# Row sums in three pieces and a routing spread over VectorE's gaps, in an RWKV attention and mixture-of-experts kernel

## The chip, the cores and the metric

The kernel runs on one core of a Trainium2 chip. The metric is the device time of one execution in microseconds (us); lower is better.

## The reference

An RWKV attention of 4 batches, 8 heads, 768 steps and head dimension 48 feeds a mixture of 8 experts, of which each row takes one.

```python
for t in range(S):                      # B, H, S, D = 4, 8, 768, 48
    cur = einsum('bhd,bhe->bhde', u[None] * k[t], v[t])
    y[t] = einsum('bhd,bhde->bhe', r[t], state + cur)
    state = w[t][..., None] * state + einsum('bhd,bhe->bhde', k[t], v[t])
x = y as (3072, 384) rows
logits = x @ w_gate + modality_bias[modality_id]
e_idx = argmax(logits); gate = softmax(logits)[e_idx]
out[row] = gate[row] * (relu(x[row] @ w1[e_idx]) @ w2[e_idx])     # 384 -> 1024 -> 384
```

## The kernel before

The attention works in 24 units of 128 steps, six for each batch. `att_iter(i)` writes one software-pipelined iteration: VectorE prepares keys and rows of unit a = i+2, TensorE makes scores and state of unit m = i+1 and outputs of unit z = i, and the finished rows of unit z-1 are added up and carried on. The tile framework schedules by hand here (`manual_schedule`): the order in which the program issues instructions is the order of each engine's queue, and the framework adds the semaphores.

In one iteration VectorE runs, in this order: a scan over the decays backwards (`scan(pp, -1)`, L356), the row sum (`x_rows`, `x_add`, L525: output pY of unit z-1 plus the diagonal term dV, 128x384, into `xp`), K of unit a (`spread`, L330), a reciprocal and a copy of four columns (L405, L406), the scan forwards, R of unit a (L330, both in `rows_op`), and the mask of the scores (L449, pS into A).

TensorE runs: transposes of K (`k_turn`, L420) unless unit m is the last of its batch; transposes of the rows of unit z-2 (`x_halves`, L550); the scores pS (L447); `delta(m)` (L342, the diagonal term, which ends with ScalarE's copy dT, L344); the state pU (L470) unless m is the last of its batch; `logits(z-2)` (L555); the state's part of the output pY (L490) unless z is the first of its batch; the unit's own part (L501). Where m is the last of its batch, the logits stand behind L490.

ScalarE copies the transposed keys (KT, L423) and rows (xT, L435), copies dT, makes half of dV (L377), scales the state (L473) and copies it to SPb (L476). GpSimd makes products of the inputs (L293, L298, L310) and the other half of dV (L370).

There is one buffer each for pS, pY and pK. The bank `T["R"]` (pR in the page) is shared: its first 192 columns hold the logits of all units, behind them stand the routing's columns, and from column 504 on the output of delta.

The routing goes in two parts, of 10 and 14 units (`PART`). The first runs inside the attention: `route_a(0)` is a generator of six VectorE operations on logits (L596 to L606), `route_x` ScalarE's exponential, `route_b` the matmuls that count rows, then `place` (positions of six units, L642), the sum of the exponentials (L637) and its reciprocal (L638), and `table(0)`. They are started from a list `hooks`, one entry an iteration, in iterations 11 to 14; a hook's VectorE operations come behind the iteration's mask. For units n with `far(n)`, which are 10 to 13 (`PART[0] <= n <= SCATTER`), the row sum is done in another way: ScalarE copies pY to `xp` (L536) and GpSimd adds dV in place (L525); that falls in iterations 11 to 14.

From iteration 15 on GpSimd scatters the routed rows (L759), in iteration 20 SP loads the first block of rows, and behind the attention the expert blocks follow.

Of the kernel before, what the change touches and what calls it, by code (L numbers as in the profile page):

```python
# [18 lines left out]
P = 128  # L19
# [50 lines left out]
NPW = 3  # L70
LOAD = SCATTER + 1 + NEAR
# [3 lines left out]
def kernel(ctx: ExitStack, tc: tile.TileContext, rkw, vt, wf, cst, mid, wg, bias, w1, w2, out):  # L75
# [270 lines left out]
    hooks = []  # L346
# [11 lines left out]
    def rows_op(a):  # L358
        step["second", a - 2] = scan(pw[a % NPW], 1)
        spread(a, "R", ins[a % NIN][:, 0:512], 1, 3)  # L360
# [11 lines left out]
    def att_iter(i):  # L372
# [28 lines left out]
        if ok(z - 1) and not far(z - 1):  # L401
            x_rows(z - 1)
        if ok(a):
            spread(a, "K", t[:, 512:1024], 3)
            nc.vector.reciprocal(out=pp[:, 1:n:SEG], in_=BE[:, 2:n:SEG])  # L405
            nc.vector.tensor_copy(out=W, in_=BE[:, 2:n:SEG])  # L406
        if i == NU - 1:
            blk_turn(0, (2,))
# [32 lines left out]
        if ok(m):  # L441
            A = wt(m, "A", [P, 2, 4, P])
            pS = pq.tile([P, 2, 4, P], F32, tag="pS", name=f"pS_{m}")
            for p in range(4):
                for hh in range(2):
                    q = slice(64 * hh, 64 * hh + 64)
                    nc.tensor.matmul(out=pS[:, hh, p], lhsT=K[q, p], rhs=R[q, p], start=True, stop=True)  # L447
            a2 = lambda v: v.rearrange("p a b c -> p (a b) c")
            step["mask", i] = nc.vector.tensor_tensor(out=a2(A), in0=a2(pS), in1=mask[:, None, :].to_broadcast([P, H, P]), op=ALU.mult)  # L449
            if i == -1:  # L450
                rows_op(a)
            if m == 0:
                k_turn()
                k_copy()
            delta(m)
            if m == 0:
                warm(NWARM[2])
# [20 lines left out]
        if ok(z - 2) and not late:  # L478
            logits(z - 2)
# [17 lines left out]
        if ok(z):  # L497
            for h in range(H):
                p, hh = divmod(h, 2)
                for q in (0, 64):  # L500
                    nc.tensor.matmul(out=pY[q:q + 64, h * D:(h + 1) * D], lhsT=A[:, hh, p, q:q + 64], rhs=v[:, h * D:(h + 1) * D],  # L501
                                     start=(first(z) and h == 0), stop=True, skip_group_check=True)
        if i == NU - 2:
# [17 lines left out]
    def far(n):  # L521
        return PART[0] <= n <= SCATTER

    def x_add(n, eng, y):
        eng.tensor_tensor(out=T["xb", n][:, 0:DM], in0=y, in1=T["dV", n].rearrange("p a b -> p (a b)"), op=ALU.add)  # L525

    def x_rows(n, eng=None):
# [5 lines left out]
        if eng is None:  # L533
            x_add(n, nc.vector, y)
# [54 lines left out]
    def route_a(c):  # L589
# [6 lines left out]
        nc.vector.scalar_tensor_tensor(out=lg, in0=lg, scalar=-1.0, in1=biasT[:, units(c)], op0=ALU.mult, op1=ALU.subtract)  # L596
        mx = wt(c, "mx", [P, NMOST], 1)[:, 0:n]
        nc.vector.tensor_reduce(out=mx, in_=lg, axis=AX.X, op=ALU.min)
        nc.vector.tensor_tensor(out=rcol(C_RK, n, E + 1)[:, :, 1:E + 1], in0=lg, in1=mx[:, :, None].to_broadcast(sh), op=ALU.is_equal)
        yield  # L600
        eq, flat = rcol(C_RK, n, E + 1), lambda t: t[:, 0:n].rearrange("p a b -> p (a b)")
        nc.vector.tensor_tensor_scan(out=flat(seen), data0=flat(same), data1=rcol(C_RK, n * (E + 1)), initial=0.0, op0=ALU.mult, op1=ALU.max)
        oh = T["oh", c] = wt(c, "oh", [P, NMOST, E], 2, BF16)[:, 0:n]
# [13 lines left out]
    def route_b(c):  # L617
# [16 lines left out]
        if c == 0:  # L634
            place(0, NEAR)
        sm = wt(c, "sm", [P, NMOST, 1], 1)[:, 0:n]
        nc.vector.tensor_reduce(out=sm, in_=ex[:, 0:n], axis=AX.X, op=ALU.add)  # L637
        nc.vector.reciprocal(out=T["xp", c][:, :, DM:DM + 1], in_=sm)  # L638
# [303 lines left out]
    for i in range(-2, NU):  # L942
# [5 lines left out]
        if i == PART[0] + 1:  # L948
            ra, tb = route_a(0), table(0)
            hooks.extend([lambda: next(ra), lambda: [*ra], lambda: hook_b(0), lambda: [*tb]])  # L950
# [55 lines left out]
    x_rows(NU - 1)  # L1006
# [259 lines left out]
```

## Time and profile before

| | |
|---|---|
| median of 3 runs | 333.1 us (332.62 to 334.82) |
| profiled execution | 335.17 us, span 333.4 us |
| mean granted TensorE clock | 0.997 |
| busy share of the span: PE, PEld, DVE, ACT, POOL | 96%, 89%, 71%, 62%, 48% |
| DVE row sums in `x_add` | 20, each 128x384 |
| attention, until the first expert matmul | 0 to 118.72 us of the span |

PE is TensorE's matmuls, PEld its weight loads, DVE is VectorE, ACT ScalarE, POOL GpSimd and SP the engine that issues loads. Times in rows are microseconds from the span's start. A row of a timeline has the start, the duration, the engine, the line and operation, output <- inputs, and the count of merged instructions; in brackets is idle time ahead of it and what ended it. The pitch of two rows is the difference of their starts. Ends of matmuls are modelled.

### The profile page before, as it was taken

Reading aid. Unit: us, or ns where it says so; the run is one execution under the profiler, and the core shown is the slowest. Engines: PE = TensorE matmul, PEld = TensorE weight load, DVE = VectorE, ACT = ScalarE, POOL = GpSimd, SP = SyncE. Lnnn points to the kernel's source line nnn. Section 1 sums busy time; section 2 is a strip of 40 time slices with the busy share of each in tenths; the row PEclk is TensorE's granted clock in tenths of the full one; section 3 lists DMA queues with packets and bytes.
Section 4 is the critical chain, followed back from the end, with each engine's and each line's share of the span. In section 5 each row is a group of like instructions: output and inputs, shape, how many; then the busy total and the mean of one; then the engine's idle time right before and its main releaser. Section 6 shows DMA issues by size and latency. Waiting matters only on the chain.

```text
span 333.4 us, 10270 instructions
## 1 busy us (share of the span) xinstructions
PE 321.6 (96%) x3917; PEld 297.6 (89%) x3917; DVE 236.2 (71%) x508; ACT 206.3 (62%) x516; POOL 159.6 (48%) x196
## 2 busy tenths in 40 slices
PE   7999999999999999999799999999999999999993
PEld 3689999889999987899589999999999988999982
DVE  7999999999999684794459758858258445815510
ACT  1687688687799893552359456956956944614420
POOL 7899999999998177065561200210210220121031
PEclk9999999999999999999999999999999999999998
DMA  7998988888984702426844800540650653210011
GB/s 237 397 297 273 272 271 280 267 256 253 283 255 133 154 3 95 97 95 237 247 158 122 261 24 2 121 162 2 128 182 3 209 129 96 94 73 21 0 32 55
DMA packets 38735, 52.31 MB, mean 157 GB/s; under 512 B 19189, under 2 KB 26133, under 8 KB 38676
## 3 DMA queue, kind: packets, MB, share of 16 engines
q1 hardware_dynamic: 35572, 42.09, 42.7%
q0 software_dynamic: 3104, 9.47, 7.6%
q8 instruction: 33, 0.54, 0.7%
q14 instruction: 26, 0.21, 0.3%
HBM read 55.43 MB, written 11.88 MB: 202 GB/s over the span
## 4 chain that ended last, share of the span: by engine, by line
issue 42%; PE 34%; POOL 11%; DVE 5%; POOLq 2%; DMA 2%; ACT 1%; SPq 1%; DVEq 0%
POOL out L870 7%; PE pS L447 6%; PE pY L501 5%; PE pS_u L827 5%; PE pY L490 4%; PE pR_x L342 3%; POOL xs L759 3%; PE pU L470 3%; PE pR_x L555 2%; POOLq L1075 2%; DMA cs<-cst 1%; PE pY_d L848 1%; DVE wl L288 1%; PE pR_x L142 1%; SPq L120 1%
## 5 line engine op out<-in xcount | busy, mean ns | idle before, releaser
L870 POOL DMA_INDIRECT out<-ot,xg x25 | 27.3, 1091 | 132.8 <-ACT ot L869 130.7
L832 DVE SCALAR_TENSOR_TENSOR hl<-pS_u,hh 128x512 fp32r<-128x512 f32 (+2 forms) x56 | 34.6, 619 | 64.9 <-ACT hh L831 51.2
L827 PE MATMUL pS_u<-xh,wh 128*128 128x512 f32 (+2 forms) x168 | 61.8, 368 | 1.8 <-DVE hl L832 1.8
L831 ACT ACTIVATE hh<-pS_u 128x512 fp32r<-128x512 f32 (+2 forms) x56 | 30.3, 541 | 52.1 <-PE pS_u L827 49.6
L827 PE MATMUL pS_u<-xh,wl 128*128 128x512 f32 (+2 forms) x168 | 61.4, 365 | 0.0
L288 DVE TENSOR_TENSOR wl<-raw,wh 128x768 fp32r<-128x768 f32 x52 | 48.5, 957 | 2.3 <-ACT wh L287 1.6
L287 ACT CAST wh<-raw 128x768 fp32r<-128x768 f32 (+1 forms) x60 | 44.9, 785 | 0.0
L827 PE MATMUL pS_u<-xo,wh 128*128 128x512 f32 (+2 forms) x168 | 43.4, 366 | 0.0
L848 PE MATMUL pY_d<-wh,hh 128*128 128x384 f32 x112 | 37.8, 338 | 0.0
L759 POOL DMA_INDIRECT xs<-xp,posT x24 | 26.6, 1107 | 23.5 <-DVE posT L642 19.7
L848 PE MATMUL pY_d<-wh,hl 128*128 128x384 f32 x112 | 37.7, 337 | 0.0
L848 PE MATMUL pY_d<-wl,hh 128*128 128x384 f32 x112 | 37.7, 336 | 0.0
L827 PEld LDWEIGHTS pS_u<-xh,wh 128*128 128x128 f32 x168 | 31.6, 188 | 5.4 <-DVE hl L832 2.2
L356 DVE TENSOR_TENSOR_SCAN pX_s<-pw,pX_s 128x268 f32<-128x268 f32 x48 | 34.3, 715 | 1.2 <-POOL pw L293 0.3
L827 PEld LDWEIGHTS pS_u<-xo,wh 128*128 128x128 f32 x168 | 31.0, 188 | 3.7 <-DVE xo L813 0.4
L827 PEld LDWEIGHTS pS_u<-xh,wl 128*128 128x128 f32 x168 | 31.6, 188 | 3.1
L298 POOL TENSOR_TENSOR G<-in 128x512 f32<-128x512 f32 x24 | 31.1, 1296 | 0.0
L377 ACT ACTIVATE dV<-v,dT 128x48 f32<-128x48 f32 x120 | 29.7, 327 | 0.2 <-POOL dV L370 0.2
L449 DVE TENSOR_TENSOR A<-pS,cs 128x1024 f32<-128x1024 f32 x24 | 29.2, 1218 | 0.6 <-PE pS L447 0.6
L447 PE MATMUL pS<-R,K 64*128 64x128 f32 x384 | 27.2, 281 | 1.4 <-DVE R L324 1.1
L310 POOL TENSOR_TENSOR in<-in 128x512 f32<-128x512 f32 (+1 forms) x23 | 28.2, 1227 | 0.6
L848 PE MATMUL pX_d<-wh,hh 128*128 128x384 f32 x80 | 27.0, 338 | 0.0
(322 smaller groups left out, 667.4 us busy)
## 6 DMA issues: line engine op xcount, KB each, us to landing
raw<-w SPq DMA_DIRECT2D x24, 768.0 KB
in<-rkw SPq DMA_DIRECT2D x66, 256.0 KB
v<-vt SPq DMA_DIRECT2D x24, 192.0 KB
wg<-wf SPq DMA_DIRECT2D x8, 576.0 KB
raw<-w SPq DMA_DIRECT2D x16, 192.0 KB
xs<-zt SPq DMA_DIRECT2D x12, 193.0 KB
xq<-xs SPq DMA_DIRECT2D x12, 192.0 KB
xq<-xs SPq DMA_DIRECT2D x12, 144.0 KB
```

What stands on the lines that cost most here:

```text
L287: nc.scalar.copy(out=wh[k][:, sl], in_=raw[k][:, sl])
L288: (eng or (nc.vector, nc.gpsimd)[k]).tensor_tensor(out=wl[k][:, sl], in0=raw[k][:, sl], in1=wh[k][:, sl].bitcast(F32), op=ALU.subtract)
L298: nc.gpsimd.tensor_tensor(out=G, in0=t[:, 0:512], in1=t[:, 512:1024], op=ALU.mult)
L356: return nc.vector.tensor_tensor_scan(out=BE[:, ::way], data0=pp[:, ::way], data1=d1[:, ::way], initial=0.0, op0=ALU.mult, op1=ALU.max)
L377: nc.scalar.activation(out=dV[:, h], in_=v0[:, h], func=AF.Copy, scale=dT[:, h:h + 1])
L447: nc.tensor.matmul(out=pS[:, hh, p], lhsT=K[q, p], rhs=R[q, p], start=True, stop=True)
L759: rows_apart("xs", nc.gpsimd.indirect_dma_start(out=xs[:, :], out_offset=bass.IndirectOffsetOnAxis(ap=posT[:, n:n + 1], axis=0), in_=T["xb ...
L827: nc.tensor.matmul(out=pp, lhsT=wsrc[0][:, g, c * P:(c + 1) * P], rhs=xsrc[:, c, 0:w], start=(n == 0), stop=(n == 3 * KC - 1))
L831: nc.scalar.activation(out=hh, in_=pp, func=AF.Relu)
L832: nc.vector.scalar_tensor_tensor(out=hl, in0=pp, scalar=0.0, in1=hh.bitcast(F32), op0=ALU.max, op1=ALU.subtract)
L848: nc.tensor.matmul(out=X["y", q, j][0:r1 - r0], lhsT=hsrc[:, r0:r1], rhs=wsrc[1][:, f], start=(f == 0 and n == 0), stop=(f == FC - 1 and n ...
L870: ins = nc.gpsimd.indirect_dma_start(out=out[:, :], out_offset=bass.IndirectOffsetOnAxis(ap=xg[0:m, j, 1:2].bitcast(I32), axis=0), in_=ot[ ...
```

## The change

1. The row sum of 384 columns is cut in three pieces of 128 (`XCUTS`). `x_third` issues one piece at each of three places: behind the first scan, ahead of the second scan (behind the reciprocal and the copy), and behind the second scan. The last two iterations, which prepare no further unit, keep the whole sum.
2. `far` becomes `PART[0] < n <= SCATTER`: unit 10's sum goes back to VectorE, in pieces; units 11 to 13 stay with ScalarE and GpSimd.
3. In iterations 12 to 14, where VectorE has no row sum, nine operations of the first routing take the three places (`slots`): in 12 the three up to the comparison, in 13 the scan, the one-hot and the subtraction, in 14 the positions, the sum and the reciprocal. The hooks of iterations 11 and 12 become empty; `route_b` (now matmuls alone for the first part) and the table keep theirs.
4. In those iterations `delta(m)` and `logits(z - 2)` are issued at the end, behind L501.

```diff
@@
+XCUTS = tuple((c, c + P) for c in range(0, DM, P))
...
@@ def rows_op(a):
         step["second", a - 2] = scan(pw[a % NPW], 1)
+        x_third(2)
         spread(a, "R", ins[a % NIN][:, 0:512], 1, 3)
@@ def att_iter(i):
         if ok(z - 1) and not far(z - 1):
-            x_rows(z - 1)
+            thirds.extend(x_rows(z - 1, cuts=XCUTS if ok(a) else ((0, DM),)))
+        if i in slots:
+            thirds.extend(slots[i])
+        x_third(0)
         if ok(a):
             spread(a, "K", t[:, 512:1024], 3)
             nc.vector.reciprocal(out=pp[:, 1:n:SEG], in_=BE[:, 2:n:SEG])
             nc.vector.tensor_copy(out=W, in_=BE[:, 2:n:SEG])
+            x_third(1)
...
-            delta(m)
+            if i not in slots:
+                delta(m)
...
-        if ok(z - 2) and not late:
+        if ok(z - 2) and not late and i not in slots:
             logits(z - 2)
...
+        if i in slots:
+            delta(m)
+            logits(z - 2)
         if i == NU - 2:
...
     def far(n):
-        return PART[0] <= n <= SCATTER
+        return PART[0] < n <= SCATTER
...
+    thirds = []
+
+    def x_third(k):
+        if thirds:
+            thirds.pop(0)()
...
         if eng is None:
-            x_add(n, nc.vector, y)
+            return [functools.partial(x_add, n, nc.vector, y, *c) for c in cuts]
...
@@ def route_a(c):
         nc.vector.scalar_tensor_tensor(out=lg, in0=lg, scalar=-1.0, in1=biasT[:, units(c)], op0=ALU.mult, op1=ALU.subtract)
+        if c == 0:
+            yield
         mx = wt(c, "mx", [P, NMOST], 1)[:, 0:n]
         nc.vector.tensor_reduce(out=mx, in_=lg, axis=AX.X, op=ALU.min)
+        if c == 0:
+            yield
...
         nc.vector.tensor_tensor_scan(out=flat(seen), data0=flat(same), data1=rcol(C_RK, n * (E + 1)), initial=0.0, op0=ALU.mult, op1=ALU.max)
+        if c == 0:
+            yield
...
@@ def route_b(c):
-        if c == 0:
-            place(0, NEAR)
-        sm = wt(c, "sm", [P, NMOST, 1], 1)[:, 0:n]
-        nc.vector.tensor_reduce(out=sm, in_=ex[:, 0:n], axis=AX.X, op=ALU.add)
-        nc.vector.reciprocal(out=T["xp", c][:, :, DM:DM + 1], in_=sm)
+        if c:
+            gates_sum(c)
+            gates_put(c)
...
@@
             ra, tb = route_a(0), table(0)
-            hooks.extend([lambda: next(ra), lambda: [*ra], lambda: hook_b(0), lambda: [*tb]])
+            hooks.extend([lambda: None] * 2 + [lambda: hook_b(0), lambda: [*tb]])
+            for k in range(2):
+                slots[i + 1 + k] = [functools.partial(next, ra)] * 3
+            slots[SCATTER + 1] = [functools.partial(place, 0, NEAR), functools.partial(gates_sum, 0), functools.partial(gates_put, 0)]
```

`gates_sum` and `gates_put` hold the sum of the exponentials and its reciprocal, which stood in `route_b`.

## Rows read from the trace of the kernel before

**Rows 1.** The timeline of VectorE, iteration 10 and the scan that opens iteration 11.
```profile
57.10 0.71 DVE L356 TENSOR_TENSOR_SCAN pX_s<-pw,pX_s 128x268 f32<-128x268 f32 x1
57.72 0.54 DVE L525 TENSOR_TENSOR xp<-pY,dV 128x384 f32<-128x384 f32 x1
58.18 0.68 DVE L330 TENSOR_TENSOR K<-in,pX_s 128x512 f32<-128x512 f32 x1
58.77 0.18 DVE L405 RECIPROCAL pw<-pX_s 128x4 f32<-128x4 f32 x1
58.86 0.13 DVE L406 COPY W<-pX_s 128x4 f32<-128x4 f32 x1
59.03 0.72 DVE L356 TENSOR_TENSOR_SCAN pX_s<-pw,pX_s 128x268 f32<-128x268 f32 x1
59.78 0.69 DVE L330 TENSOR_TENSOR R<-in,pX_s 128x512 f32<-128x512 f32 x1
60.39 1.22 DVE L449 TENSOR_TENSOR A<-pS,cs 128x1024 f32<-128x1024 f32 x1
61.52 0.71 DVE L356 TENSOR_TENSOR_SCAN pX_s<-pw,pX_s 128x268 f32<-128x268 f32 x1
```
**Rows 2.** The timeline of TensorE, iteration 7 and the scores of iteration 8.
```profile
43.98 1.16 PE L447 MATMUL pS<-R,K 64*128 64x128 f32 x16 [0.24 <-DVE A L449]
...
45.56 0.65 PE L470 MATMUL pU<-v,KT 128*64 128x48 f32 x16
46.04 0.51 PE L555 MATMUL pR_x<-cs,xT 128*64 128x8 f32 x12
46.39 0.86 PE L490 MATMUL pY<-SPb,R 128*64 128x96 f32 x16
...
48.10 0.47 PE L420 MATMUL pK_('k', 9)_1162<-cs,K 64*128 64x64 f32 x8
48.40 0.35 PE L550 MATMUL pK_('k', 9)_1162<-cs,xp 64*128 64x64 f32 x6
48.59 1.11 PE L447 MATMUL pS<-R,K 64*128 64x128 f32 x16
```
**Rows 3.** The timeline of TensorE, scores and pY of iteration 10, scores of 11.
```profile
57.46 1.11 PE L447 MATMUL pS<-R,K 64*128 64x128 f32 x16
...
58.99 0.86 PE L490 MATMUL pY<-SPb,R 128*64 128x96 f32 x16
...
61.66 1.16 PE L447 MATMUL pS<-R,K 64*128 64x128 f32 x16
```
**Rows 4.** The timeline of GpSimd, its addition in iteration 11.
```profile
65.50 0.98 POOL L525 TENSOR_TENSOR xp<-xp,dV 128x384 f32<-128x384 f32 x1
```
**Rows 5.** The timeline of TensorE, iterations 12 and 13, and the scores of iteration 15.
```profile
66.54 0.41 PE L550 MATMUL pK_('k', 13)_1591<-cs,xp 64*128 64x64 f32 x6 [0.27 <-POOL xp L525]
...
71.00 0.40 PE L550 MATMUL pK_('k', 14)_1699<-cs,xp 64*128 64x64 f32 x6 [0.36 <-POOL xp L525]
...
81.06 1.11 PE L447 MATMUL pS<-R,K 64*128 64x128 f32 x16
```
**Rows 6.** The timeline of ScalarE, the KT copy of iteration 12, then iteration 13.
```profile
66.98 0.59 ACT L423 COPY KT<-pK_('k', 13)_1591 128x512 f32<-128x512 f32 x1
...
72.07 0.59 ACT L423 COPY KT<-pK_('k', 14)_1699 128x512 f32<-128x512 f32 x1
72.54 0.50 ACT L435 COPY xT<-pK_('k', 14)_1699 128x384 f32<-128x384 f32 x1
73.00 0.17 ACT L344 COPY dT<-pR_x 128x8 f32<-128x8 f32 x1
...
73.19 1.00 ACT L377 ACTIVATE dV<-v,dT 128x48 f32<-128x48 f32 x4
74.09 1.19 ACT L473 ACTIVATE pU<-pU,W 128x48 f32<-128x48 f32 x4
75.31 0.64 ACT L476 COPY SPb<-pU 64x192 f32<-64x192 f32 x2
```

More of the change, by code (lines that the diff above doesn't have):

```diff
@@ L344, in delta @@
         nc.scalar.copy(out=wt(m, "dT", [P, 4, 2]), in_=pd)
-    hooks = []
+    hooks, slots = [], {}
     done = iter(range(FC))
@@ L521, in far, with x_add, x_rows @@
     def far(n):
-        return PART[0] <= n <= SCATTER
-    def x_add(n, eng, y):
-        eng.tensor_tensor(out=T["xb", n][:, 0:DM], in0=y, in1=T["dV", n].rearrange("p a b -> p (a b)"), op=ALU.add)
-    def x_rows(n, eng=None):
+        return PART[0] < n <= SCATTER
+    def x_add(n, eng, y, c0=0, c1=DM):
+        eng.tensor_tensor(out=T["xb", n][:, c0:c1], in0=y[:, c0:c1], in1=T["dV", n].rearrange("p a b -> p (a b)")[:, c0:c1], op=ALU.add)
+    thirds = []
+    def x_third(k):
+        if thirds:
+            thirds.pop(0)()
+    def x_rows(n, eng=None, cuts=((0, DM),)):
         c = int(n >= PART[0])
@@ L633, in route_b, with gates_sum, gates_put @@
             add(pR[:, (j + 1) * E:(m + 1) * E], onesb, oh[:, j:j + 1].to_broadcast([P, m - j, E]), stop=j == n - 1)
-        if c == 0:
-            place(0, NEAR)
-        sm = wt(c, "sm", [P, NMOST, 1], 1)[:, 0:n]
-        nc.vector.tensor_reduce(out=sm, in_=ex[:, 0:n], axis=AX.X, op=ALU.add)
-        nc.vector.reciprocal(out=T["xp", c][:, :, DM:DM + 1], in_=sm)
+        if c:
+            gates_sum(c)
+            gates_put(c)
+    def gates_sum(c):
+        T["sm", c] = wt(c, "sm", [P, NMOST, 1], 1)[:, 0:PART[c]]
+        nc.vector.tensor_reduce(out=T["sm", c], in_=ex[:, 0:PART[c]], axis=AX.X, op=ALU.add)
+    def gates_put(c):
+        nc.vector.reciprocal(out=T["xp", c][:, :, DM:DM + 1], in_=T["sm", c])
     def place(n, k):
@@ L1005 @@
     q0, q1 = seq[0:2]
-    x_rows(NU - 1)
+    x_rows(NU - 1)[0]()
     at(q0, "u", 1, lambda: x_cols(NU - 2, pt(("x", 0), "pX")), lambda: x_cols(NU - 1, pt(("x", 1), "pU")))
```

## The prediction

> **What bounds the kernel now.** I read four views in this order: the busy tenths of the page, which say that TensorE is busy in nearly every slice, so that what it loses in the attention units is lost to the span; the VectorE timeline; the TensorE timeline; and the ScalarE timeline of the routing units. I count units by the loop variable i of the kernel: in i, TensorE multiplies scores for unit i+1 and outputs for unit i, and VectorE adds the rows of unit i-1.
>
> VectorE has no idle time in a unit [rows 1]: from one first scan to the next pass 4.42 us (57.10 to 61.52). The reader is to see two kinds of step there. An operation that needs nothing of the one ahead starts 0.08 to 0.10 before that one has ended (scan to row sum 0.62, though the scan lasts 0.71); one that needs it starts about 0.04 after its end (scan at 59.03, R at 59.78: 0.75). So a gap of about 0.13 follows each scan when the dependent operation comes next. The row sum already fills the first of them.
>
> TensorE is as full [rows 2]: a unit goes from 43.98 to 48.59 without a gap, 4.61, and VectorE's mask of the unit ahead releases its first matmul only now and then (0.24 idle at 43.98). Every group's modelled duration is some 0.15 longer than its pitch (0.47 against 0.30 at 48.10), so that idle stands for about 0.41 of lost pitch. From unit 7's scores at 43.98 to unit 11's at 61.66 [rows 2, 3] pass 17.68; by pitch 0.13 of it is a wait of that kind, which leaves 4.39 a unit against VectorE's 4.42. Both are the bound, and TensorE can pass on what VectorE gains only where it really waits. There are three such rows before the routing, ahead of the scores of units 5, 7 and 11, by pitch 0.15, 0.41 and 0.13: together 0.7.
>
> **The pieces.** 17 row sums on VectorE and unit 10's become 54 pieces of 128 columns. A piece's pitch: the 512-column K took 0.59 and the 384-column sum 0.46 [rows 1], so 0.13 for each 128 columns, and 0.46 less 0.26 leaves 0.19 to 0.20. The unit then runs: K at 0.62 + 0.19 = 0.81 after the scan instead of 1.08 (0.27 won); the second piece starts 0.08 after the copy and takes 0.19 before the second scan, where 0.17 stood (0.10 lost); R at 0.62 + 0.19 = 0.81 after the second scan instead of 0.75 (0.06 lost). Net 0.10 a unit, 4.32, hidden or not.
>
> The price lies elsewhere. The row sum reads pY, of which there is one buffer, and the next unit's first matmul into it (L490, or L501 in a batch's first unit) waits for the sum. It ended at 57.72 + 0.54 = 58.26 [rows 1], L490 came at 58.99 [rows 3]. Now the third piece ends 0.62 + 0.19 + 0.59 + 0.09 + 0.08 + 0.19 + 0.62 + 0.28 = 2.66 after the first scan, and with 0.05 for the semaphore (mask end 60.39 + 1.22 to matmul 61.66) that is 59.81: 0.82 after L490 wants to start. Queued behind L490 are everything else of the unit and the next unit's scores. In ordinary units L490 comes 2.41 after the scores (43.98 to 46.39 [rows 2]) and the wait is 0.0 to 0.2. In units 4, 10 and 16, where no state is made and no logits stand ahead, it comes 1.53 after them (57.46 to 58.99 [rows 3]). Unit 1 has no logits yet either: 0.4. Followed unit by unit, TensorE's start is late by 0.4 after unit 1; by 0.75 after unit 4 (0.54 of new wait less the 0.15 waited there anyway); by 0.35 at unit 7, whose 0.41 it gets back; by 0.75 after unit 10 (0.54 less 0.13). The waits are 0.54 and not 0.82 since TensorE comes there already late. From then on the first piece waits for pY, and VectorE's 0.10 a unit buys nothing.
>
> **Unit 10's rows return to VectorE.** GpSimd loses an addition of 0.98 (at 65.50) and ScalarE a copy [rows 4]. TensorE's transposes waited for that addition at 66.54 (0.27 idle, 0.44 by pitch) [rows 5]. That goes: minus 0.4, so TensorE starts unit 12's transposes at about 66.54 - 0.43 + 0.75 = 66.86, 0.3 late. The like wait at 71.00 was on the next addition, which now comes some 0.95 earlier; it is covered by what follows.
>
> **Nine routing operations in the gaps, delta and logits last.** The nine stood after the mask of units 11 to 13; in the gaps VectorE's units 12 to 14 shorten by 0.3 to 0.7. It is not VectorE that decides there. delta ends with ScalarE's copy dT, and delta, logits, dT and the nine operations all use the one bank pR. The semaphores written into the kernel before make the logits wait for dT and delta for VectorE's last access to pR. Before, the state matmuls stood between delta and logits and hid dT. Now the two stand together at the unit's end, and dT is queued on ScalarE behind all its work of the unit. What was queued on TensorE behind the logits, the key transposes and the next unit's scores, waits with them. So each of units 12, 13 and 14 becomes a loop through ScalarE, from TensorE's transposes to the next ones: 0.44 to the KT copy (66.54 to 66.98 [rows 5, 6]), 0.47 to xT and 0.46 past it, 0.90 for dV (73.19 to 74.09), 1.22 for the state's scaling, 0.66 for SPb (its 0.64 and 0.02), 0.23 for dT (0.17 and a semaphore) [rows 6], then logits 0.35 and key transposes 0.30 [rows 2]: 5.0. Unit 12 adds 0.15 for the far copy ahead of KT: 5.2. In unit 13 the scan of the routing waits for those logits, the subtraction comes two scans later, and ScalarE's exponential waits for it, with its own time some 0.8: 5.8. In unit 14 the positions wait for the logits, the mask follows 3.6 later, then two operations of the table on pR, and delta waits for these, 0.5 more than the loop: 5.5. Together 16.5. Before, the same three went from 66.54 to 81.06 - 0.19 = 80.87 [rows 5]: 14.3. Loss 2.2; TensorE starts unit 15 at 81.06 + 0.3 + 2.2 = 83.6.
>
> A rule speaks against this part. The Trainium skill, "PSUM — Partial Sum Buffer", section "PSUM bank collisions raise a hardware error", says that accesses of two engines are to be guarded by bank and quadrant, not by address, since other columns of one bank collide too. No row of before shows TensorE idle between delta and logits, as 0.48 of state matmuls lies between (45.56 to 46.04 [rows 2]), so the trace does not decide it. By address alone this part would cost nothing (second rival).
>
> Other queues: GpSimd's next G tile waits for the late delta, with within and the first scatter behind it, but GpSimd runs ahead of the users of its tiles; its copy of the row numbers moves one unit later, still ahead of the scatters; the loads on the SP queue hang on VectorE's steps and move with them. I cost these at nothing; without that cover it would be the same 1.5 that delta is late. From unit 17 on ScalarE paces TensorE, which waits for KT, and passes the lateness on unchanged.
>
> **Sum.** 0.75 - 0.4 + 2.2 = 2.5; unit 16 adds a third late unit, 0.45, of which 0.2 was waited anyway: 2.8. The profiled execution (335.17, span 333.4) would become 338.0 and 336.2; it stands 2.1 above the median of 333.1, so I forecast 333.1 + 2.8 = 335.9.
>
> **Rivals.**
> First, the third piece's wait falls outside TensorE's path (the pieces are quicker, or L490 comes later than I have it) while ScalarE's loop stands: TensorE gains its 0.7 up to unit 11, 0.4 at unit 12, loses 2.2 in the loop, 0.2 back at unit 16: plus 0.9, 334.0. For it: ordinary units differ by only 0.0 to 0.2. Against: 0.82 in unit 10. 12%.
>
> Second, logits don't have to wait for dT: 0.75 - 0.4 and the wait at 71.00 gone (0.5), unit 16 plus 0.2: about 0, 333.1. Against it are the semaphores of before. 14%.
>
> Third, neither binds: TensorE keeps 0.7 and of the 0.4 what GpSimd's next addition leaves (0.95 in all): minus 1.0, 332.1. 9%.
>
> Fourth, slower: a piece costs what a held operation costs. Its duration would be about 0.28 (0.54 less two times 0.13) and 0.04 of gap, so 0.32 instead of 0.19; VectorE's unit becomes 4.32 + 0.39 = 4.71, past 4.42, and VectorE is the bound in units 1 to 11: 11 times 0.26 = 2.9 at unit 11 instead of 0.75, and 2.9 - 0.4 + 2.2 + 0.8 (units 15 to 17) = 5.5 in all, 338.6. It decides from a piece's pitch of 0.22 on, where the unit is 4.42 again. The overlaps of 0.08 to 0.10 in [rows 1] speak against it. 10%. The Trainium skill ("VectorE: DVE Perf Modes", section "The DRAIN you can't avoid") says so, that the next operation starts only when the pipe is empty, and advises fewer operations; its next section allows operations without a wait to start earlier, and there the trace agrees (0.62 against 0.71).
>
> **How the numbers follow.** The forecast holds 52%, between 1.7 and 4.0 late: its lower end has the late units at 0.2 and the loop at 5.0 each time, its upper the full 0.82 and 6.0 in unit 13. The remaining 3% are delays that I can't name. One per cent, 3.3 us, is about what a measurement of this kernel can tell from no change (its three runs spread by 2.2). Over 336.4 lie 38% of the forecast (0.20), the fourth rival (0.10) and those delays (0.03): 0.33. Under 329.8 lies no case; I take 0.03 from the third rival, should its gain be larger than I see. The rest, 0.64, is within 1%. The range leaves out the third rival below and the fourth above: 332.6 to 337.6.
>
> **What would show it.** Right: in units 4, 10 and 16, L490 starts just behind the third piece; K comes 0.81 after the first scan; in units 12 to 14 the logits start 0.06 behind dT, with TensorE idle 0.5 to 1.7 ahead of them, and from transposes to transposes pass 5.2, 5.8 and 5.5; unit 15's scores start at 83 to 84; attention ends 2 to 3 us late and the expert blocks keep their length. Wrong: TensorE back to back from delta to logits, dT before SPb on ScalarE, or a first expert matmul ahead of 118.7.

## The result, and the profile after

The changed kernel takes 338.25 us (median of six runs, 336.57 to 341.21) against 333.97 of the kernel before: ratio 1.0137, 95% interval 1.0102 to 1.0172, or 4.6 us more where 2.8 were forecast. 338.25 lies above the range of 332.6 to 337.6. Measured once more (experiment e8) the ratio is 1.0173 (1.0147 to 1.0199), 5.8 us. The profiled execution took 338.35 us, its span is 336.5 us, and the first expert matmul comes at 124.02 instead of 118.72.

VectorE's timeline, iteration 7 of the changed kernel, answers to [rows 1]:

```profile
45.78 0.71 DVE L357 TENSOR_TENSOR_SCAN pX_s<-pw,pX_s 128x268 f32<-128x268 f32 x1
46.40 0.27 DVE L535 TENSOR_TENSOR xp<-pY,dV 128x128 f32<-128x128 f32 x1
46.59 0.68 DVE L331 TENSOR_TENSOR K<-in,pX_s 128x512 f32<-128x512 f32 x1
...
47.27 0.13 DVE L411 COPY W<-pX_s 128x4 f32<-128x4 f32 x1
47.32 0.28 DVE L535 TENSOR_TENSOR xp<-pY,dV 128x128 f32<-128x128 f32 x1
47.52 0.71 DVE L357 TENSOR_TENSOR_SCAN pX_s<-pw,pX_s 128x268 f32<-128x268 f32 x1
48.14 0.27 DVE L535 TENSOR_TENSOR xp<-pY,dV 128x128 f32<-128x128 f32 x1
48.33 0.67 DVE L331 TENSOR_TENSOR R<-in,pX_s 128x512 f32<-128x512 f32 x1
...
50.06 0.71 DVE L357 TENSOR_TENSOR_SCAN pX_s<-pw,pX_s 128x268 f32<-128x268 f32 x1
51.23 0.29 DVE L535 TENSOR_TENSOR xp<-pY,dV 128x128 f32<-128x128 f32 x1 [0.46 <-PE pY L508]
```

The pieces are what they were forecast to be: pitch 0.19 to 0.20, K 0.81 after the scan instead of 1.08, and 4.28 us in a unit that waits for nothing, where 4.42 stood. Nothing comes of it: in the next unit the first piece already waits 0.46 for TensorE's pY (last row), and TensorE itself has come late because of where the third piece stands. TensorE's timeline, units 1 to 4 (units are counted by i, as in the prediction):

```profile
20.26 0.88 PE L497 MATMUL pY<-SPb,R 128*64 128x96 f32 x16 [0.54 <-DVE xp L535]
...
25.28 0.28 PE L571 MATMUL pR_x<-cs,xT 128*64 128x8 f32 x3 [0.34 <-issue]
...
31.17 0.88 PE L497 MATMUL pY<-SPb,R 128*64 128x96 f32 x16 [0.71 <-issue]
...
33.14 1.11 PE L453 MATMUL pS<-R,K 64*128 64x128 f32 x16
35.25 0.88 PE L497 MATMUL pY<-SPb,R 128*64 128x96 f32 x16 [0.44 <-DVE xp L535]
```

and the same places in the kernel before, without idle time:

```profile
19.31 0.85 PE L490 MATMUL pY<-SPb,R 128*64 128x96 f32 x16
...
30.81 1.11 PE L447 MATMUL pS<-R,K 64*128 64x128 f32 x16
...
32.34 0.86 PE L490 MATMUL pY<-SPb,R 128*64 128x96 f32 x16
```

The reader is to see two kinds of idle time. 0.54 and 0.44 are waits for the third piece, in units 1 and 4 as forecast (they come again at 62.52 and 92.67, 0.45 each, in units 10 and 16). 0.34 and 0.71 carry no semaphore ("issue"); the first one cuts a group of twelve matmuls in two, and the copy that all twelve read (xT, one operation) was there for the first nine. The last section shows that both fall where TensorE enters a new block of its own instructions, called its code below. Unit 4's scores start at 33.14, 2.3 late.

TensorE's timeline, units 12 to 14, answers to [rows 5]; behind it ScalarE's, which answers to [rows 6]:

```profile
69.48 0.35 PE L566 MATMUL pK_('k', 13)_1612<-cs,xp 64*128 64x64 f32 x6
...
74.00 0.52 PE L571 MATMUL pR_x<-cs,xT 128*64 128x8 f32 x12 [1.20 <-ACT dT L345]
74.75 0.35 PE L566 MATMUL pK_('k', 14)_1720<-cs,xp 64*128 64x64 f32 x6
...
79.77 0.52 PE L571 MATMUL pR_x<-cs,xT 128*64 128x8 f32 x12 [0.51 <-ACT dT L345]
80.52 0.35 PE L566 MATMUL pK_('k', 15)_1848<-cs,xp 64*128 64x64 f32 x6
...
84.40 0.63 PE L343 MATMUL pR_x<-cs,G 128*64 128x2 f32 x16 [0.39 <-DVE hit L728]
85.30 0.52 PE L571 MATMUL pR_x<-cs,xT 128*64 128x8 f32 x12 [0.27 <-ACT dT L345]
86.05 0.35 PE L566 MATMUL pK_('k', 16)_1962<-cs,xp 64*128 64x64 f32 x6
```

```profile
73.12 0.64 ACT L483 COPY SPb<-pU 64x192 f32<-64x192 f32 x2
73.79 0.17 ACT L345 COPY dT<-pR_x 128x8 f32<-128x8 f32 x1
...
78.89 0.64 ACT L483 COPY SPb<-pU 64x192 f32<-64x192 f32 x2
79.55 0.17 ACT L345 COPY dT<-pR_x 128x8 f32<-128x8 f32 x1
```

The logits wait for dT, and dT stands behind SPb on ScalarE. From transposes to transposes pass 5.27, 5.77 and 5.53, together 16.57; forecast were 5.2, 5.8 and 5.5. The transposes of unit 12 no longer wait for GpSimd (but see e4: they don't there either, with unit 10's sum still on GpSimd).

### The profile page after: what moved, and what is told of

Read it like the earlier page. It is cut to its first block, busy times and chain, and to the rows that moved or that the text cites. A ratio compares the mean times of both kernels' runs of the same rounds, so it can differ in the third digit from the quotient of the medians.

```text
span 336.5 us, 10312 instructions
## 1 busy us (share of the span) xinstructions
PE 321.6 (96%) x3917; PEld 297.9 (89%) x3917; DVE 236.5 (70%) x545; ACT 205.8 (61%) x515; POOL 159.4 (47%) x195
## 4 chain that ended last, share of the span: by engine, by line
issue 41%; PE 28%; POOL 10%; DMA 6%; DVE 6%; ACT 4%; POOLq 2%; SPq 1%; DVEq 0%; ACTq 0%
PE pS_u L854 6%; POOL out L897 6%; DMA in<-rkw 5%; PE pY L508 3%; PE pS L453 3%; PE pY L497 3%; PE pY_d L875 3%; PE pX_d L875 2%; POOL xs L786 2%; DVE K L331 2%; PE pR_x L571 2%; DVE pX_s L357 2%; ACT dV L379 2%; PE pR_x L343 2%; POOLq L1105 2%
## 5 line engine op out<-in xcount | busy, mean ns | idle before, releaser
L875 PE MATMUL pY_d<-wh,hh 128*128 128x384 f32 x112 | 37.8, 337 | 0.0
```

Source lines behind the costliest of these rows:

```text
L875: nc.tensor.matmul(out=X["y", q, j][0:r1 - r0], lhsT=hsrc[:, r0:r1], rhs=wsrc[1][:, f], start=(f == 0 and n == 0), stop=(f == FC - 1 and n ...
```

## The experiments

The kernels were timed in groups, each on one chip; a time is the ratio to the kernel before on the same chip, with its 95% interval, and us over it (the ratio less one, times that group's median of before: 335.88 for e1 to e4, 335.75 for e5 to e8, 333.09 for e9 to e12, 335.68 for e13 to e15). The intervals reach 0.6 to 1.2 us to either side (e9's and e12's 1.5), so smaller differences between two kernels are not shown. The other columns are rows of TensorE's timeline, one execution each: start of unit 4's and unit 12's scores, the time from unit 12's to unit 15's scores (the three loops), and the first expert matmul.

| kernel | unit 4 | unit 12 | loops | expert | ratio | us over |
|---|---|---|---|---|---|---|
| before | 30.81 | 66.77 | 14.29 | 118.72 | | |
| before, again (e16) | 31.05 | 67.00 | 14.30 | 119.07 | | |
| changed | 33.14 | 69.67 | 16.57 | 124.02 | 1.0137 (1.0102 to 1.0172) | 4.6 |
| changed, again (e8) | 33.07 | 68.94 | 16.57 | 124.80 | 1.0173 (1.0147 to 1.0199) | 5.8 |
| changed, e17 | 32.87 | 69.08 | 17.60 | 125.90 | | |
| changed, e18 | 32.12 | 67.99 | 17.83 | 124.82 | | |
| e1 | 32.67 | 69.31 | 13.94 | 121.97 | 1.0043 (1.0019 to 1.0067) | 1.4 |
| e2 | 30.97 | 66.44 | 17.87 | 122.08 | 1.0053 (1.0025 to 1.0082) | 1.8 |
| e3 | 31.03 | 66.49 | 14.54 | 120.29 | 0.9999 (0.9976 to 1.0022) | 0.0 |
| e4 | 32.41 | 68.28 | 13.97 | 121.55 | 1.0041 (1.0016 to 1.0067) | 1.4 |
| e5 | 31.73 | 67.78 | 14.77 | 121.40 | 1.0050 (1.0019 to 1.0081) | 1.7 |
| e6 | 31.20 | 66.66 | 15.23 | 120.81 | 1.0029 (1.0010 to 1.0047) | 1.0 |
| e7 | 32.77 | 67.56 | 17.72 | 123.36 | 1.0091 (1.0067 to 1.0115) | 3.1 |
| e9 | 31.01 | 66.89 | 20.05 | 124.10 | 1.0133 (1.0086 to 1.0179) | 4.4 |
| e10 | 31.02 | 67.29 | 14.01 | 119.30 | 1.0020 (1.0002 to 1.0038) | 0.7 |
| e11 | 32.24 | 67.51 | 14.32 | 119.75 | 1.0004 (0.9976 to 1.0033) | 0.1 |
| e12 | 30.95 | 67.22 | 16.56 | 121.56 | 1.0107 (1.0062 to 1.0153) | 3.6 |
| e13 | 31.11 | 67.59 | 14.33 | 121.31 | 1.0038 (1.0013 to 1.0064) | 1.3 |
| e14 | 32.18 | 68.10 | 13.95 | 121.82 | 1.0060 (1.0035 to 1.0085) | 2.0 |
| e15 | 32.53 | 69.12 | 15.07 | 122.88 | 1.0072 (1.0047 to 1.0097) | 2.4 |

### Each part alone, and each undone

**e1**, from the changed kernel: delta and logits at their places.

```diff
-            if i not in slots:
-                delta(m)
+            delta(m)
...
-        if ok(z - 2) and not late and i not in slots:
+        if ok(z - 2) and not late:
...
-        if i in slots:
-            delta(m)
-            logits(z - 2)
```

> The changed kernel with delta and logits of units 12 to 14 put back at their places in the unit; the pieces and unit 10 on VectorE stay. Theory (the loop through logits, transposes, piece and scan costs 2.2 us over three units, and the early stretch 1.6 us more than forecast): the loops from transposes to transposes fall from 5.27, 5.77 and 5.53 us to about 4.5, 5.3 and 4.6, the first expert matmul comes 2 us earlier than 124.02, and the time is 1.5 to 2.5 us below the changed kernel's, so about 2 to 3 us above the kernel before. Rival (the price sits in the early stretch alone and units 12 to 14 are late for another reason): within 0.7 us of the changed kernel's time. The program is the same as the changed kernel's up to unit 12, so its first units also say whether the stops of TensorE that no semaphore explains (0.34 at 25.28, 0.71 at 31.17, 0.45 at 46.73) come again: if they belong to the pieces, scores of unit 10 start at 60.4 again; if to the one execution, near 58.8.

The loops fall to 13.94, and 1.4 us over before remain, less than the 2 to 3 expected: the late pair carries most of the change's price. A stop without a semaphore comes again at the same matmul as in the changed kernel (30.70, 1.12 idle).

**e2**, from the changed kernel: the row sum whole, at the first place.

```diff
-            thirds.extend(x_rows(z - 1, cuts=XCUTS if ok(a) else ((0, DM),)))
+            thirds.extend(x_rows(z - 1, cuts=((0, DM),)))
```

> The changed kernel with the row sum whole, at the place of the first piece; unit 10 on VectorE and the late delta and logits stay. Theory (the third piece costs what TensorE waits for it, 0.45 to 0.54 us in units 1, 4, 10 and 16, and little else): about 1 us below the changed kernel, and no wait of pY for VectorE in those units. Rival (the whole early delay of 2.9 us by unit 10 comes from the pieces, the unexplained stops of TensorE too): scores of unit 10 start near 57.5 as before, and the time is 2.6 us or more below the changed kernel, so about 2 us above the kernel before, which would be the price of the late logits alone.

Units 4 to 12 run as in before, no wait for VectorE's sum, no stop ahead of 100 us: the whole early delay belongs to the pieces, as the rival said. 1.8 us remain.

**e3**, from the kernel before: unit 10 back on VectorE, whole (the far line of the change alone).

> The kernel before with unit 10's row sum whole on VectorE instead of GpSimd, and nothing else of the change. Theory: the transposes of unit 12 no longer wait for GpSimd's add, 0.4 us; the loop behind it starts earlier and the time is 0 to 0.9 us below the kernel before. Rival (VectorE's unit is longer by the sum, 0.33 us, and scores of unit 11 are late by that): 0 to 0.4 us above.

```profile
66.49 1.12 PE L447 MATMUL pS<-R,K 64*128 64x128 f32 x16
70.23 0.40 PE L550 MATMUL pK_('k', 14)_1698<-cs,xp 64*128 64x64 f32 x6
71.14 1.16 PE L447 MATMUL pS<-R,K 64*128 64x128 f32 x16 [0.50 <-DVE A L449]
```

In these rows of TensorE, unit 12 starts 0.3 earlier and no transposes wait for GpSimd; then unit 13's scores wait 0.50 for VectorE's mask, which ends at 71.09 (70.69 and 70.93 in the two traces of before). The gain is given back one unit later: 0.0 us (0.8 less to 0.7 more).

**e4**, from the kernel before: the pieces alone (`XCUTS`, `x_third` and its three places).

> The kernel before with the row sum in three pieces and nothing else of the change: unit 10's sum stays on GpSimd, delta and logits keep their places. Theory (0.75 us in TensorE's start of unit 10 and 0.25 in unit 16): 0.8 to 1.2 us above the kernel before. Rival (the pieces carry the unexplained stops as well): scores of unit 10 start 2.5 to 3 us later than 57.46 and the time is 2.5 us or more above the kernel before. Second rival (pieces are free, and only the late logits cost): within 0.5 us.

1.4 us, a little over the expected 0.8 to 1.2. Unit 4 is 1.5 late, and from unit 4 to unit 10 pass 26.60 us as in before (26.65): what unit 4's wait of 0.45 costs is got back on the way, as forecast. Unit 10's wait lengthens the way to unit 11's scores from 4.20 to 4.69, but from there to unit 12's pass 4.58 instead of 5.11: TensorE comes so late that its transposes (68.09, no idle time) don't wait for GpSimd's addition, though unit 10's sum is still there.

**e6**, from the changed kernel: both e1's and e2's edits, so that unit 10 and the nine routing operations in the gaps remain.

> The changed kernel without the pieces and without the late delta and logits: what is left is unit 10's row sum on VectorE and the split of hooks. By the two calls' sums (pieces 1.4, late logits 1.8, unit 10 nothing): the time of the kernel before within 0.8 us. Theory of the prediction (unit 10 alone gives back 0.4): 0.2 to 0.8 us below the kernel before. No stop of TensorE that no semaphore explains before unit 10; its fetches of code (256 instructions each) start within 2 us of TensorE's crossing into the block ahead, as in the kernel before, where those of the kernels with pieces start 3.4 to 3.6 us after it at the second and the third.

1.0 us, a little above the 0.8 expected: delta waits 1.22 us at 68.99 for a routing operation on bank pR that now stands in a gap ahead of it. The gaps need the late delta. That the late pair costs more than this wait (1.8 in e2 against 1.0) is likely, but not clear of the two intervals.

**e9**, from the kernel before: delta and logits last in units 12 to 14 alone, the routing operations where they were.

```diff
-            delta(m)
+            if i not in (12, 13, 14):
+                delta(m)
...
-        if ok(z - 2) and not late:
+        if ok(z - 2) and not late and i not in (12, 13, 14):
             logits(z - 2)
...
+        if i in (12, 13, 14):
+            delta(m)
+            logits(z - 2)
```

> The kernel before with delta and logits of units 12 to 14 last in their units and nothing else: row sums whole, unit 10's on GpSimd, the nine operations of routing where they were. Theory (late logits cost 2.2 us over the three loops): score starts of units 12 to 16 span 2 to 2.7 us more than the 18.76 of the kernel before, and the time is 1.8 to 2.7 us above it. Rival (late logits cost only together with the pieces, which the two medians of the changed kernel against the kernel with the sum whole suggest): 0 to 1 us above.

```profile
66.89 1.11 PE L447 MATMUL pS<-R,K 64*128 64x128 f32 x16
...
71.73 0.68 PE L342 MATMUL pR_x<-cs,G 128*64 128x2 f32 x16 [2.19 <-DVE pR_x L610]
72.67 0.82 PE L559 MATMUL pR_x<-cs,xT 128*64 128x8 f32 x12 [0.26 <-ACT dT L344]
...
74.22 2.02 PE L447 MATMUL pS<-R,K 64*128 64x128 f32 x16
```

4.4 us, beyond both expectations. A late delta meets the routing's operations behind the mask (2.19 us for L610), and the sixteen score matmuls behind that wait take 2.02 us instead of 1.11: this was the first sign of a slower clock (below).

### Which of the two late steps

**e5** has e1's first edit alone (delta at its place, logits last), **e15** its second alone (logits at their place, delta last).

> The changed kernel with delta back at its place in units 12 to 14, logits still last. Theory (logits are late because they wait for dT, 1.20, 0.51 and 0.27 us, and dT is late because delta is): those waits are gone, the three loops from transposes to transposes sum to about 14.8 us instead of 16.57, and the time is 1.2 to 2 us below the changed kernel's of this call. Rival (the last place alone sets it, since routing's chain to the transposes starts at the logits wherever delta stands): the sum of the loops stays above 15.8 and less than 0.8 us comes back.

> The changed kernel with logits of units 12 to 14 back at their place, delta still last. Theory of the prediction (logits last wait for dT, which delta's late place makes late): without logits behind delta nothing of the path waits for dT in the same unit, 1.5 to 2.5 us below the changed kernel, so 2.5 to 4 above the kernel before. Rival (delta's late place costs by itself, since dV and with it pY of the next units wait for dT): within 1 us of the changed kernel, 4 to 6 us above the kernel before.

The loops take 14.77 (as e5's theory expected) and 15.07, against 13.94 with neither and 16.57 with both. In neither do the logits of the three units wait for dT; what is left are waits on the same bank, 0.35 and 0.60 of delta for the routing (e5) and 0.73 of the logits for ScalarE's exponential (e15). The times are 1.7 and 2.4 us over before, against 1.4 with neither and 5.8 for the changed kernel in e5's group. So most of the price is that of the pair: logits right behind delta wait for dT. e5 gives back 4.1 us, twice what was expected; its loops account for 1.8, unit 12's scores start another 1.2 earlier than in e8, and the rest is open.

### What of the pieces

**e7**, from the changed kernel: two pieces, 256 columns at the first place and 128 at the second.

```diff
-            thirds.extend(x_rows(z - 1, cuts=XCUTS if ok(a) else ((0, DM),)))
+            thirds.extend(x_rows(z - 1, cuts=((0, 2 * P), (2 * P, DM)) if ok(a) else ((0, DM),)))
```

> The changed kernel with two pieces instead of three: 256 columns at the first place, 128 at the second, none behind the second scan; so the sum ends about 0.8 us earlier in the unit. Theory (TensorE waits for the end of the sum, 0.45 to 0.54 us in units 1, 4, 10 and 16): those waits are gone and the time is 0.6 to 1.2 us below the changed kernel's of this call. Rival (what costs is the splitting itself, the sums pushed into gaps that VectorE doesn't have, or the late fetches of code that go with it): scores of unit 10 start within 0.5 us of the changed kernel's, and the time within 0.5 us.

No pY waits for VectorE any more, and the time is 2.7 us less than the changed kernel's in the same group; yet unit 4 is still late (32.77), with stops of 0.50 and 0.44 that no semaphore explains. More came back than the theory allows, and the rival fell too.

**e10** and **e11** have e4's pieces from unit 5 on, and up to unit 4; **e12** is the changed kernel with the pieces from unit 5 on (`XCUTS if ok(a) and i > 4`, or `i < 5`).

> The pieces alone on the kernel before, but only from unit 5 on; units 1 to 4 keep the whole sum. Theory (the price of the pieces is paid in units 1 to 4, where TensorE waits for the third piece in unit 1 and then for code; the waits of 0.45 us in units 10 and 16 are hidden, since scores of unit 4 to unit 10 took 26.60 us with pieces and 26.65 without): within 0.4 us of the kernel before; the second and the third fetch of code start less than 2.2 us after TensorE crosses into the block ahead. Rival (what the prediction said: 0.75 us where unit 10 is late, 0.25 in unit 16): 0.7 to 1.2 us above the kernel before.

> The other half: the pieces alone on the kernel before, in units 1 to 4, and the whole sum from unit 5 on. Theory (the price is paid there): 1 to 1.8 us above the kernel before, as the kernel with the pieces in all units (1.4); scores of unit 4 start 1.2 us or more after 30.81, the second and third fetch of code start 2.8 us or more after the crossing. Rival (the prediction's: unit 10 and unit 16): 0 to 0.4 us above.

> The changed kernel with the sum whole in units 1 to 4 and in pieces from unit 5 on. Theory (of the changed kernel's 4.6 to 6 us, some 1.8 are paid for the pieces in units 1 to 4, the rest for the late delta and logits): 2 to 3.5 us above the kernel before. Rival (pieces and late logits cost more together than each alone, wherever the pieces stand): above 4 us still.

The theory that units 1 to 4 carry the price is not borne out, though the intervals just touch it. e11 is 1.3 late at unit 4, as expected, but 0.6 at unit 12 (from unit 4 to unit 12 pass 35.27 us, in before 35.96) and 0.1 us over in time (0.8 less to 1.1 more); e10's 0.7 (0.1 to 1.3) is at the edge of the prediction's own figure (unit 10 and unit 16). e12 is 3.6, between the two expectations, and its interval (2.1 to 5.1) reaches into both.

**e13** puts e4's three pieces together at the first place, **e14** the whole sum at the third.

> The kernel before with the row sum cut in three pieces that all stand at the first place, behind the first scan; unit 10 on GpSimd, routing, delta and logits as before. Theory (what costs is that the last piece ends late, behind the second scan, so that TensorE waits in unit 1 and is late with what follows): no wait of pY for VectorE, scores of unit 4 within 0.4 us of 30.81, time within 0.6 us of the kernel before. Rival (the splitting costs: 36 more operations, late fetches of code): second and third fetch of code 2.8 us or more after the crossing, scores of unit 4 1 us or more late, 0.8 to 1.6 us above the kernel before.

> The kernel before with the row sum whole, at the third place, behind the second scan; nothing else changed. Theory (the late end of the sum costs): the sum ends some 0.25 us later than the third piece did, pY waits 0.6 to 0.8 us for it in units 1, 4, 10 and 16, the fetches of code are late as with the pieces, scores of unit 4 start 1.2 us or more after 30.81, and the time is 1 to 2 us above the kernel before. Rival (the splitting costs): within 0.6 us of the kernel before.

e13 has no late unit 4 and no stop before 100 us: the early delay comes from the later place, not from cutting. But its time is 1.3 over, more than the 0.6 expected. Three pieces in a row lengthen VectorE's unit from 4.42 to 4.55 us, and scores wait for the mask, which makes 0.7 at unit 12; another 1.7 is lost behind unit 15 and stays open. Two of the waits:

```profile
44.76 1.16 PE L452 MATMUL pS<-R,K 64*128 64x128 f32 x16 [0.41 <-DVE A L454]
...
72.04 1.16 PE L452 MATMUL pS<-R,K 64*128 64x128 f32 x16 [0.35 <-DVE A L454]
```

e14 waits for the sum in units 1, 10 and 16 (0.58, 0.66, 0.84) and costs 2.0. Cutting and placing late each cost by themselves; the pieces as built (1.4) are no sum of the two.

### Repeats

> The changed kernel again, unaltered, on the chip of these runs. If its parts add (pieces 1.4, late logits 1.8, unit 10 nothing, each measured against the kernel before in the first call): 3.2 us above the kernel before, ratio near 1.0095. If the first measurement holds (ratio 1.0137): 4.6 us above, and the parts together cost 1.4 us more than each alone. In its trace: if the late fetches of code belong to the pieces, the second and third fetch start 3 us or more after TensorE crosses into the block ahead, and TensorE stops at its 962nd instruction again; if to one execution, only one or none of them.

> The kernel before again, for a second trace. Expected: scores of unit 4, 10, 12 and 16 start within 0.3 us of 30.81, 57.46, 66.77 and 85.53, no stop of TensorE for code before unit 10; the first expert matmul 0.5 to 1.5 us later than 118.72, since the stretch from unit 16 to it took 33.19 us there and 33.2 to 34.8 in the other kernels.

> The changed kernel unaltered, a third trace. Theory (behind the wait of 1.0 to 1.2 us for dT in unit 12 the clock falls in most executions): where the mean granted clock is 0.994 or less, the stretch of 3 us behind that wait shows a granted clock of 0.5 to 0.8, score starts of units 12 to 14 span 1 to 2 us more than the 11.04 of both traces so far, and the rest of the attention gives part of it back. Rival (the low mean clock of the timed executions comes from the expert part, as in the kernel before): the clock in units 12 to 15 is 1.00 and the low stretch lies behind 124 us.

> The same kernel once more, a fourth trace, since one execution may fall on either kind. The same two readings: granted clock of 0.5 to 0.8 in the 3 us behind unit 12's wait for dT, or 1.00 there and the low stretch in the expert part. In both cases the stops for code at TensorE's instructions 706 and 962 are expected again, 0.3 to 0.7 us each, as in the first two traces.

e8 confirms the size. The parts measured alone (1.4, 1.8, 0.0) make 3.2, give or take 1.5: clearly less than e8's 5.8, not clearly less than the first 4.6. e16 shows the one trace of before to be typical; its first expert matmul, expected 0.5 to 1.5 later, is 0.35 later. e18 has none of the stops for code that were expected again, e17 one of 0.07 and one of 0.71. e17 and e18 found what the first two traces of the changed kernel did not have. The view by stretches of e17 (stretch, TensorE's busy time, granted clock, DMA share, GB/s):

```profile
69.00:72.00 3.00, 3.00 (x88) 1.00 0.89 283
72.00:75.00 3.00, 2.00 (x46) 0.97 0.86 285
75.00:78.00 3.00, 3.00 (x43) 0.50 0.65 180
78.00:81.00 3.00, 2.74 (x81) 0.96 0.69 226
```

and of the first trace of the changed kernel:

```profile
72.00:75.00 3.00, 1.80 (x58) 1.00 0.89 306
75.00:78.00 3.00, 3.00 (x74) 1.00 0.63 180
```

Behind unit 12's logits, which waited 1.00 us for dT, the clock falls to 0.50 of 2.4 GHz, its lower level, for some 3 us. That loop takes 7.05 instead of 5.77, the three 17.60. e18 shows the same (0.58 and 0.85 in the two stretches from 72 on, loops 17.83), e2, e7 and e9 too. That the rest of the attention would give part of it back was expected and did not come: unit 15's scores to the experts take 39.2 and 39.0 us in e17 and e18, 37.8 and 39.3 in the other two.

## Why the prediction was too low

The direction held, and so did the two mechanisms that were priced as losses: TensorE's wait for the third piece and the loop through ScalarE. What failed is two terms that the sum put at nothing (TensorE's stops for its own code, and a lower clock behind a wait) and unit 10's gain. Lateness of TensorE, as forecast and as the mean of the changed kernel's four traces less the mean of before's two (the forecast's 0.75 "after unit 4" stands behind that unit's wait, so it is read at unit 5's scores):

| at | forecast | measured |
|---|---|---|
| unit 2's scores | 0.4 | 0.8 |
| unit 4's scores | 0.4 | 1.9 |
| unit 5's scores | 0.75 | 2.3 |
| unit 11's scores | 0.75 | 2.5 |
| unit 12's scores | 0.3 | 2.0 |
| unit 15's scores | 2.5 | 4.9 |
| first expert matmul | 2.8 | 6.0 |
| end of the span | 2.8 | 4.6 |

**The pieces.** Right: their pitch, VectorE's unit (4.28 against 4.32), which units wait for the third piece, and how long (0.41 to 0.56 in the four traces, forecast 0.4 to 0.54). The step that failed is the sum behind it, "Followed unit by unit, TensorE's start is late by 0.4 after unit 1; by 0.75 after unit 4". It knows no other wait to speak of (0.0 to 0.2 in ordinary units), and between unit 2's and unit 4's scores, where it loses nothing, 1.05 us are lost on average (1.4, 1.5, 1.1 and 0.1): TensorE stops for its own code, with 0.34 and 0.71 idle in the first trace, 0.49 and 0.71, 0.07 and 0.71, and none in e18. By pitch a stop costs some 0.18 more than its idle time, as the prediction itself says of such rows. The other 0.4 of the excess stand in unit 1: its third piece costs 0.6 by pitch instead of 0.4, and its scores start 0.2 late behind VectorE's mask. Alone the pieces cost 1.4 (0.5 to 2.3) where the sum had 1.0, so this time alone would not have shown the step to be wrong.

**Unit 10, "minus 0.4".** Failed: e3 measures 0.0, and the rows show why. In e3, where TensorE is not late, the wait for GpSimd goes, and VectorE's mask takes the gain back in unit 13; I had looked one wait ahead and not two. In e4, where TensorE is late, the wait is gone with the sum still on GpSimd. The fall of the lateness from 2.5 at unit 11 to 2.0 at unit 12 looks like the forecast gain and comes without it.

**Delta and logits last, "loss 2.2".** The loop through ScalarE was right to 0.1 at full clock (16.57 against 16.5; before 14.3), unit by unit as well, and the steps are those forecast: VectorE waits 1.30 for the logits in unit 13 (scan at 74.64) and 1.45 in unit 14 (positions at 80.41). e5 and e15 show the cause to be the one given, logits behind delta waiting for dT. What was left out is the clock: in two of four traces TensorE's idle time ahead of those logits is followed by the lower level, and the loops cost 3.3 and 3.5 instead of 2.3. The timed runs say that this is common: the median of their mean granted clocks is 0.9925 and 0.9905 for the changed kernel and 0.9905 to 0.993 for the four others with the pair late, against 0.9955 to 0.998 for all kernels without it, before included. In before's runs beside e13 to e15 (28 of 29, without one that is 5.5 us off) time rises by 0.29 us for each 0.001 that the clock falls, in the changed kernel's own two sets of six runs by 0.27 and 0.13, so I estimate 0.5 to 1.7 us for the 0.004 to 0.006.

**Unit 16 and after, 0.25.** From unit 15 to the experts the changed kernel loses 1.1. Its traces show the expected 0.45 in unit 16, then stops for code or waits for dT of 0.4 to 0.7 in other places each time; e3 and e13, whose loops are those of before, take 39.3 and 39.4 us for this stretch as well, against 37.7 in before. This part is left open. The prediction let ScalarE pass the lateness on "unchanged" here, which failed.

**The expert part**, forecast unchanged, takes 214.6 and 214.5 us in before's two traces and 212.5, 214.7, 213.0 and 212.8 in the changed kernel's four. That is no gain of the change: a wait for hl of 1.3 to 1.9 us at 165 to 171 stands in both traces of before, in e8, e1 to e7 and e13 to e15, and is missing in all of e9 to e12 (212.3 to 212.6) as in the three others. So the end of the span is no measure of the attention here, and the row of the first expert matmul is the better one.

**The rivals.** The second and third (logits need not wait for dT) are refuted by the rows above. The first asked for pieces off the path; e4 and e10 speak against it. The fourth came nearest by its time (5.5) and is wrong in its mechanism: a piece's pitch is 0.19, not 0.32. Its time is luck, and its own sum slips: 4.71 less 4.42 is 0.29 a unit and not 0.26.

By the traces, 2.0 at unit 12, 2.3 for the loops, 0.6 for the clock (1.0 and 1.3 in two of four) and 1.1 behind unit 15 make the 6.0 at the first expert matmul. By time the parts don't close as well: 1.4 for the pieces and 2.3 for the loops are 3.7, while e8's two runs at a mean clock of 0.999 are still 4.2 and 5.5 over before, so the clock can't be all of the rest. Open remain what is lost behind unit 15, whether the pair really costs so much less beside whole sums (e2 less e6: 0.8 us, with intervals of 1.0 and 0.6) although its loops are as long there, and why code mostly comes late where a part of the sum stands at a later place.

## What to carry to other kernels

An operation cut up to fill gaps is finished when its last piece is: look who waits for the end, not how much shorter the engine's own stretch becomes. A wait that goes away is a gain only where nothing else holds the same step: look one wait further, and at whether the step will be late anyway. Two matmul groups that share a PSUM bank with a copy between them want other work between them too; moving both to the unit's end turned 0.2 us of copy into a loop through everything queued ahead of it. And a new wait of a microsecond on TensorE should be priced twice, by its length and by the clock that may follow it, and looked for in several executions, since the first two traces here showed none.

## What the runs showed of the hardware

**TensorE's code comes in blocks by DMA, and can be late.** In the attention units of every trace one packet of 16 KB on an instruction queue (q8) stands against each 256 of TensorE's recorded instructions (matmuls, weight loads and waits), and the stops "issue" at 25.28, 31.17 and 46.73 fall on instructions 706, 962 and 1730, a multiple of 256 apart, whatever matmul that is. (Three later stops without a releaser fall elsewhere, in e4, e8 and e13 at 102 to 107 us, all ahead of pU; they are not counted as code.) Over the first 21 packets of all 20 traces of this study TensorE enters a block 1.18 us after its packet's end at the earliest, and at these three stops 1.35 to 1.39. In the changed kernel it enters the block ahead of the first stop's at 19.32; the DMA view from 19.3 to 22.8 has no packet of q8,

```profile
DMA packets 535, 0.96 MB, mean 273 GB/s; under 512 B 67, under 2 KB 75, under 8 KB 535
...
q1 hardware_dynamic: 535, 0.96, 83.3%
```

and the one from 22.8 to 23.2 has one:

```profile
q8 instruction: 1, 0.02, 15.4%
```

The packet lasts from 22.94 to 23.93, and TensorE goes on at 25.28. The Trainium skill, "Advanced Engine Details and Errata", section "ISA Cache", gives a cache line of 16 KB, which it counts as 256 instructions; the packets here agree. Packets start after TensorE's crossing into the block ahead, in us, for the second and the third block of the attention:

| sum in units 1 to 4 | kernels | second | third |
|---|---|---|---|
| whole, or three pieces, at the first place | before twice, e2, e3, e6, e9, e10, e12, e13 | 0.9 to 1.7 | 0.9 to 2.5 |
| with a part at the second or third place | changed four times, e1, e4, e5, e7, e11, e15 | 2.9 to 3.6 (once 0.9) | 2.7 to 3.8 |
| whole, at the third place | e14 | 1.5 | 3.2 |

What holds the packet back isn't settled: SP issues its loads at the same times within 0.15 us in e3 (fetch 1.5 after the crossing) and e4 (3.4), from 17.07 to 21.79. Nor is the place of the sum enough: e18 is the changed kernel, and its second packet comes after 0.9.

**The clock follows idle time of 1 us, but not always.** Behind waits of 1.00 (e17), 1.19 (e2, e7, e18) and 2.19 us (e9) it fell to its lower level for 3 to 7 us; behind waits of 1.20 and 0.99 at the same place in the changed kernel's first two traces, and 1.19 in e12, it did not. In the expert part, behind the wait for hl of 1.3 to 1.9 us that thirteen traces have, before's two among them, it fell in one (e1, at 169.7, where that part takes 216.1 us instead of 214.7). The Trainium skill, "TensorE: Matmul & The Clock Gate", section "HAM oscillation — how this bites in real kernels", tells of a matmul kernel whose clock falls again behind each wait between its groups; the granted clocks here agree that a wait is what goes ahead of the fall.
